# Output rows of a recurrent attention layer: three of four TensorE transposes given to a transposing DMA, with the output products of half 1 run block by block

## The chip, the cores and the metric

The kernel runs on one core of one Trainium2 chip. The metric is the device time of one execution in microseconds (us); lower is better. A comparison with the kernel before uses several executions of both on the same chip.

## The reference

Two layer pairs are applied to `x` (1 x 2048 x 448, bf16), one after the other with the same weights. The first of a pair is attention with a recurrent memory over segments of 32 tokens, the second a gated feed-forward layer; both add to their input, and both read it through a layer norm without weights.

```
for s in range(64):                       # 64 segments of 32 tokens
    h = concat([mem, x[32*s : 32*s+32]])  # 8 memory rows + 32 tokens = 40
    q, k, v = h @ Wq, h @ Wk, h @ Wv      # 16 heads of 256
    p = softmax(mask(q k^T / 16))         # memory columns open, tokens causal
    o = (p v) @ Wo                        # 40 x 448
    mem = o[:8]                           # into the next segment
    out[32*s : 32*s+32] = o[8:]
x = x + out
x = x + (relu(norm(x) @ W_gate) * (norm(x) @ W_up)) @ W_down
```

A segment needs the memory that the segment before left, so 64 segments of one layer follow each other.

## The kernel before

**Preparation.** Before the recurrence, `Wq Wk^T` of each head is made into `A_sb` and `Wv Wo` into `B_sb`, in 28 tiles for each half (8 heads) of the heads. Scores are then `(A_sb^T h)^T h`, and the output is `B_sb` times the weighted rows `Y`.

**Steps and chains.** The main loop (L1293) runs 68 steps. In step g chain 0 does segment g of the first attention layer and chain 1 segment g - 4 of the second (LAG = 4), so from g = 4 to 63 both chains are in each product's 80 columns. The feed-forward layer works on 128 rows, 64 of each chain (class `Feed`, L590), in the odd steps from 3 on. An odd step is long and an even one short. `early` (L1073) is an odd step with both chains.

**One step** (`step`, L902). `project` (L779) multiplies `hT` (the segment's rows turned, memory included) with `A_sb` of half 0 into five banks of PSUM in the order `BANKS` (L43); each bank is copied to `TQ` or `TZ` by DVE or ACT (L814). Then half 1 in the same way. `scores` (L931) makes memory scores (Sm) and token scores (Sx) of a half, `softmax` (L828) spreads their work over DVE and ACT as small closures (`[0]` first, `[1]` exp, `[2]` second, `[3]` lift, `[4]` peak, `[5]` rest), and writes the probabilities to `PJ`. They are turned either on TensorE (`flipped`, L873, tile pps) or by a DMA (`fetched`, L881, tile PT). `weigh_m` (L976) and `weigh_x` (L989) make `Y` of the memory rows and of the tokens, from the probabilities and `hk`, the segment's rows in their natural order. `hk` is itself a transposing DMA of `hT` (`turn_columns`, L893: two DMAs and a copy on POOL). `project_out` (L1023) multiplies `Y` with `B_sb` into `ox`, three blocks of 128 output columns, with the blocks inside the loop over the 28 tiles; `project_last` (L1031) makes the last 64 columns (o3). `finish` (L1056) copies the new memory from `ox` into `hT` of the next step and the token rows into `OT`. Behind it come the next step's early products (`project_early`, L764), which need only the last 64 columns, then `weigh_x` of half 0, then the first bank. `weigh_x` of half 1 runs inside the next step.

**Rows into the feed-forward layer.** `OT` holds the output with its columns on the partitions, in four blocks. In the odd step, behind the products of the first bank, `flip_rows` (L601) turns the four blocks on TensorE into the tile otp, `residual` (L606) adds them to `xa` on DVE and starts the row statistics, `norm` (L628) centres them into xn, `fetch` (L638) turns xn into `xT` by a DMA, and `squares` (L631) makes the row scale that `down_out` uses. `open_rows` (L647) is the first reader of `xT`.

**Order.** The wrappers at L85 and L100 keep each engine's instructions in the order in which the code emits them; only semaphores decide when. SP issues nearly all DMAs, in order. PSUM has eight banks; `bank` (L125) takes the one that a running estimate says has been free longest. In short steps with g % 4 = 2 (up to 54), `norm_rows` (L306) puts row statistics of later input rows on DVE between the copies of `project_last` and those of `finish`.

**The end.** After the loop the last 64 rows of the second layer are made in rows straight away (tile ot, L1309 to L1315), in two banks: even and odd tiles each fill one half of the array with 448 columns. `residual_of` (L610) copies one bank by ACT and adds it to the other by DVE.

Of the kernel before, what the change touches and what calls it, by code (L numbers as in the profile page):

```python
# [15 lines left out]
DM = 448  # L16
# [48 lines left out]
def build_kernel(ctx, tc, A_x, A_mem0, A_Wq, A_Wk, A_Wv, A_Wo, B_W_gate, B_W_up, B_W_down, out,  # L65
# [515 lines left out]
    nc.gpsimd.memset(OT[:], 0.0)  # L581
    xT = main.tile([P, 4, 128], BF, name="xT")
# [7 lines left out]
    class Feed:  # L590
# [188 lines left out]
    def project(hf, chains, hb, j, banks, pre={}, busy=False, first=None, inside=None, head=0, between=None):  # L779

        n = L * len(chains)
        for i0, k in banks:
# [110 lines left out]
    def turn_columns(g):  # L893

        if columns_by_dma(g):
            hk = HK[g % 2]
            src = hTb[g // BLK % 2][:, g % BLK, :]
            sp.dma_start_transpose(hk[:, 0:3, :], src[:, 0:3 * HI])
            sp.dma_start_transpose(hk[:, 3:4, 0:64], src[0:64, 3 * HI:HW])
            pool.tensor_copy(hk[:, 4, 64:128], hk[:, 3, 0:64])  # L900

    def step(g, ff, pre, late):  # L902
# [9 lines left out]
        end = g == nsteps - 1  # L912
        ox = None

        def ox_open():

            nonlocal ox
            ox = bank([P, 3, W], F32, "ox", 1400 if len(active(g + 1)) == len(chains) else 700, hold=True)
# [104 lines left out]
        def project_out(hf, t0, t1):  # L1023

            for t in range(t0, t1):
                for mc in range(3):
                    mm(ox[:, mc, lo:hi], B_sb[:, hf, t, mc * 128:(mc + 1) * 128],
                       YB[hf][:, t, lo:hi], start=(hf == 0 and t == 0 and mc == 0),
                       stop=(hf == 1 and t == NT - 1 and mc == 2), skip_group_check=True)

# [25 lines left out]
        def finish():  # L1056
            let_go(ox)
            if ms:
                src = ox[:, :, M0:M0 + 16].rearrange("p k (c m) -> p k c m", m=MEM)
                set_mem(g + 1, src[:, :, ms[0]:ms[-1] + 1, :], ms)  # L1060
            o = (g - 1) % BLK * SEG
            for c in xs:
                o2 = o + (TB if c == 0 else 0)
                dve.tensor_copy(OT[:, 0:3, o2:o2 + SEG], ox[:, :, XO[c]:XO[c] + SEG])

        def feed(*us):
            if ff is not None:
# [8 lines left out]
                between=(lambda: (ff.flip_rows(), ff.residual(), early and ff.norm())) if ff is not None else None)  # L1076
        project(0, chains, hb, j, BANKS[0][1:2], pre)
        hk = HK[g % 2] if columns_by_dma(g) else hk_make()
# [5 lines left out]
        if ff is not None:  # L1084
            if not two:
                ff.norm()
            ff.squares()
# [82 lines left out]
        if early:  # L1170
# [18 lines left out]
            px1 = fetched(PX[1], "x1")  # L1189
            ff.down()  # L1190
# [44 lines left out]
        else:  # L1235
# [7 lines left out]
            short = two and len(xs) == 1  # L1243
            if two:
                x1[3]()
            if not short:
                x0[0]()
                x0[1]()
            late_flip = NT if short else 23
            project_out(0, 0, late_flip)  # L1250
            pm = flipped(PM[1], 1, "m1") if ms else None
# [8 lines left out]
            straight = g <= LAG  # L1260
            if not straight:
                px0 = fetched(PX[0], "x0")
# [10 lines left out]
            flip = 25 if short else 10  # L1273
            project_out(1, 0, flip)
            if straight:
                px0 = flipped(PX[0], 2, "x0", act)
            project_out(1, flip, 25)
            next_piece()
            project_out(1, 25, NT)
# [29 lines left out]
    ot = [bank([P, 512], F32, "ot") for _ in range(2)]  # L1309
    mm(ot[0][0:TB, 0:DM], ident[:, 0:TB], ff.x[:], start=True, stop=False, tile_position=(0, 0), skip_group_check=True)  # L1310
# [78 lines left out]
```

## Time and profile before

| | us |
|---|---|
| median of 3 runs | 1521.43 |
| lowest, highest | 1520.22, 1522.34 |
| the profiled execution | 1520.04 |
| its span on the core | 1518.3 |

The profile is of one execution. PE is TensorE's matmuls, PEld its weight loads, DVE is VectorE, ACT ScalarE, POOL GpSimd, SP SyncE. A group's row reads: line, engine, operation, out<-in, shapes and count, then busy time in us, mean ns of one, idle time before it and what ended most of that idle time. A timeline row reads: start in us, length, engine, line, operation, count, and in brackets the idle time before it. Nearly all rows have line L107, L148 or L156, those of the wrappers, so tiles tell them apart. Matmuls overlap: a row's length runs to the end of its last one, and pace is read from one row's start to the next row's start. SPq rows are DMA issues; their length is the time that SP was held.

### The profile page before, as it was taken

To read this page: it belongs to the slowest core of one execution; us is meant where nothing else is said; L and a number is where in the kernel's file an instruction comes from. 1 tells how busy PE (TensorE), PEld (TensorE's weight loads), DVE (VectorE), ACT (ScalarE), POOL (GpSimd) and SP (SyncE) were. 2 spreads that over 40 slices of the span, in tenths; PEclk is the share of its full clock that TensorE was granted. 3 is DMA by queue.
4 is the path that set the end of the run, shared out by engine and by line. 5 is a ranking of instruction groups with operands and counts; after the bars stand their busy time and mean duration, and the time that the engine had idled before them with its cause. 6 is when DMAs were issued, how large, how long until landed. Compare 5 with 4: busy or idle time off the path is not lost.

```text
span 1518.3 us, 88540 instructions
## 1 busy us (share of the span) xinstructions
PE 1506.4 (99%) x40112; PEld 1396.0 (92%) x40112; DVE 1054.9 (69%) x3499; ACT 710.2 (47%) x1952; POOL 117.6 (8%) x234
## 2 busy tenths in 40 slices
PE   9999999999999999999999999999999999999998
PEld 6699999999999999999999999999999999999997
DVE  7766766777666677766677677666767776666664
ACT  6744444454444444544444445444444454444443
POOL 3301010101010010001001010100001000000000
PEclk9999999999999999999999999999999999999999
DMA  8721111111111111111111111111111111111100
GB/s 246 247 55 29 25 28 35 24 33 28 33 26 31 28 29 30 27 32 29 33 23 28 34 25 33 27 36 23 30 31 27 32 27 31 27 24 25 27 20 16
DMA packets 146250, 60.51 MB, mean 40 GB/s; under 512 B 119241, under 2 KB 144977, under 8 KB 145873
## 3 DMA queue, kind: packets, MB, share of 16 engines
q1 hardware_dynamic: 143744, 50.66, 14.6%
q8 instruction: 314, 5.14, 1.4%
q0 software_dynamic: 1088, 3.68, 0.7%
q14 instruction: 64, 0.52, 0.1%
q10 hardware_dynamic: 1040, 0.52, 0.1%
HBM read 23.18 MB, written 3.80 MB: 18 GB/s over the span
## 4 chain that ended last, share of the span: by engine, by line
PE 96%; DMA 3%; DVE 1%; issue 0%; ACT 0%; POOLq 0%; POOL 0%; SPq 0%; ACTq 0%
PE prj L148 32%; PE ox L148 25%; PE gps L148 6%; PE ups L148 6%; PE dps L148 6%; PE o L148 4%; PE y L148 4%; PE Sx L148 3%; DMA PT<-PJ 2%; PE Sm L148 1%; PE bps L148 1%; PE ya L148 1%; PE aps L148 1%; PE tpw L156 1%; PE yb L148 1%; PE otp L156 0%
## 5 line engine op out<-in xcount | busy, mean ns | idle before, releaser
L148 PE MATMUL prj<-hT,A_sb 128*128 128x80 bf16 (+3 forms) x15232 | 538.6, 199 | 0.4
L148 PEld LDWEIGHTS <-A_sb 128*128 128x128 bf16 (+1 forms) x15232 | 498.9, 99 | 20.8 <-issue 0.8
L148 PEld LDWEIGHTS <-B_sb 128*128 128x128 bf16 (+1 forms) x15008 | 472.5, 103 | 9.7 <-issue 2.1
L148 PE MATMUL ox<-Y,B_sb 128*128 128x80 bf16 (+2 forms) x11256 | 417.0, 200 | 1.5 <-issue 1.4
L107 ACT CAST Y<-y 128x128 bf16<-128x128 f32 (+2 forms) x452 | 150.3, 410 | 207.5 <-PE y L148 201.7
L107 ACT CAST TQ<-prj 128x480 bf16<-128x480 f32 (+1 forms) x380 | 184.5, 497 | 95.4 <-PE prj L148 83.8
L107 DVE CAST Y<-y 128x256 bf16<-128x256 f32 (+2 forms) x316 | 135.5, 479 | 42.5 <-PE y L148 42.0
L107 ACT ACTIVATE se<-se 128x160 f32<-128x160 f32 (+2 forms) x270 | 81.5, 302 | 166.4 <-DVE se L107 155.9
L148 PEld LDWEIGHTS <-Wg_sb 128*128 128x128 bf16 (+2 forms) x2128 | 124.5, 97 | 9.8 <-issue 2.7
L107 DVE CAST TQ<-prj 128x480 bf16<-128x480 f32 (+1 forms) x228 | 125.6, 572 | 8.0 <-PE prj L148 7.5
L148 PE MATMUL gps<-xT,Wg_sb 128*128 128x128 bf16 (+3 forms) x1904 | 128.7, 215 | 0.0
L148 PEld LDWEIGHTS <-hk 128*128 128x128 bf16 (+2 forms) x1950 | 101.0, 96 | 15.9 <-DMA PT<-PJ 2.8
L148 PE MATMUL ups<-xT,Wu_sb 128*128 128x128 bf16 (+3 forms) x1632 | 108.5, 215 | 0.4 <-DVE xT L107 0.4
L148 PEld LDWEIGHTS <-Wu_sb 128*128 128x128 bf16 (+1 forms) x1904 | 105.1, 97 | 1.7 <-issue 0.2
L107 ACT CAST TZ<-prj 64x320 bf16<-64x320 f32 (+2 forms) x264 | 96.5, 376 | 20.0 <-DVE TZ L107 16.0
L107 DVE TENSOR_REDUCE ssum<-se 128x4 f32<-128x160 f32 (+2 forms) x270 | 73.3, 271 | 42.1 <-ACT se L107 38.5
L107 DVE SCALAR_TENSOR_TENSOR hh<-gps,ut 128x512 bf16<-128x512 f32 (+2 forms) x136 | 80.4, 593 | 31.8 <-ACT ut L107 30.1
L148 PE MATMUL dps<-Wd_sb,hh 128*128 128x448 bf16 (+1 forms) x504 | 93.6, 342 | 0.8 <-DVE hh L107 0.7
L148 PEld LDWEIGHTS <-TQ 128*128 128x128 bf16 x1938 | 85.3, 96 | 4.6 <-ACT TQ L107 1.5
L148 PE MATMUL y<-PT,hk 40*128 40x256 bf16 (+3 forms) x1280 | 85.8, 248 | 1.7 <-DMA PT<-PJ 1.6
L107 DVE TENSOR_TENSOR PJ<-se,rs 128x160 bf16<-128x160 f32 (+2 forms) x270 | 76.1, 282 | 9.6 <-DVE rs L107 0.3
L107 ACT COPY os<-o 64x16 f32<-64x16 f32 (+3 forms) x134 | 25.7, 191 | 121.9 <-PE o L148 120.2
(142 smaller groups left out, 1612.5 us busy)
## 6 DMA issues: line engine op xcount, KB each, us to landing
wo<-in_A_Wo_dram POOLq DMA_DIRECT2D x8, 448.0 KB, 5.5
nat<-in_A_Wv_dram SPq DMA_DIRECT2D x8, 384.0 KB, 5.2
PT<-PJ SPq DMA_TRANSPOSE x160, 2.4
nat<-in_A_Wq_dram SPq DMA_DIRECT2D x6, 384.0 KB, 4.9
nat<-in_A_Wk_dram SPq DMA_DIRECT2D x6, 384.0 KB, 5.4
hk<-hT SPq DMA_TRANSPOSE x132, 3.1
dx<-ahead SPq DMA_DIRECT2D x15, 128.0 KB, 2.7
xp<-in_A_x_dram SPq DMA_DIRECT2D x16, 112.0 KB, 2.9
```

Of the source, the lines that this page charges most:

```text
L107: r = f(*a, **k)
L148: in_order(nc.tensor.matmul(out, lhsT, rhs, **k))
L156: in_order(nc.tensor.transpose(out, src, idn))
```

## The change

In the even steps from 4 to 62 (`turning`), half 1's output products run block by block: all 28 tiles of columns 128 to 255, then 256 to 383, then 0 to 127. The first two of these blocks have a PSUM tile of their own (ox2). When they are done, ACT copies their token rows to `OT`, one transposing DMA turns blocks 1 to 3 of `OT` (columns 128 to 447, with the 64 that project_last left) into the new tile `OR`, and DVE copies their memory rows to `hT`; then come the products of block 0. In the odd step behind it TensorE turns block 0 alone, and the residual is added in two parts, behind the copy of the first bank. The fetch of `xT` is issued ahead of the second bank and no longer behind the third, `squares` behind the softmax of half 1's tokens, and one TQ copy goes from DVE to ACT.

In short steps with both chains on both sides (`whole`) the exponential of x0 is emitted behind the turn of m1, x0's probabilities are written and fetched before x1's maximum, and ACT does the copies of m1's PT and of ya. The turn of m1 comes after 21 tiles of half 0 and no longer after 23. In steps 64 and 66 x0 is turned on TensorE and no longer by a DMA. POOL's copy for `hk` is emitted behind the second bank. At the end, each tile's product is split into two halves of 224 columns side by side in one bank, and ACT and DVE each copy one half to `xa`.

```diff
+        def flip_first(self):
+            self.rows = bank([P, 128], BF, "otp")
+            tr(self.rows[:], OT[:, 0, :], ident[:])
+
+        def residual_rows(self):
+            dve.tensor_tensor(self.x[:, 128:DM], OR[:].rearrange("p k d -> p (k d)")[:, 0:DM - 128], self.x[:, 128:DM],
+                              op=ALU.add)
+            dve.tensor_tensor(self.x[:, 0:128], self.rows[:], self.x[:, 0:128], op=ALU.add)
+            self.statistics(self.first)
...
         def residual_of(self, ot):
-            odd = main.tile([P, DM], F32, tag="odd", name="odd")
-            act.copy(odd[0:TB, :], ot[1][TB:P, 0:DM])
-            dve.tensor_tensor(self.x[0:TB, :], ot[0][0:TB, 0:DM], odd[0:TB, :], op=ALU.add)
+            for eng, r, cols in zip((dve, act), FR, HALF):
+                evac(eng, self.x[0:TB, cols], ot[r, 0:DM // 2])
...
-                copies(act if (i0 != 6 if busy and hf else i0 % 12) else dve, slice(0, P), T)
+                copies(act if (i0 != 6 if busy and hf else i0 if early else i0 % 12) else dve, slice(0, P), T)
...
+        turning = ff is None and g >= LAG and len(active(g + 1)) == 2
...
+            if turning:
+                a = bank([P, 1, W], F32, "ox", after, hold=True)
+                b = bank([P, 2, W], F32, "ox2", 700, hold=True)
+                ox = ((a, 0), (b, 0), (b, 1))
...
+        def project_out_rows(first):
+            o = (g - 1) % BLK * SEG
+            for mc in (1, 2, 0):
+                if mc == 0:
+                    src = ox[1][0]
+                    let_go(src)
+                    for c in xs:
+                        o2 = o + (TB if c == 0 else 0)
+                        act.copy(OT[:, 1:3, o2:o2 + SEG], src[:, :, XO[c]:XO[c] + SEG])
+                    sp.dma_start_transpose(OR[:], OT[:, 1:4, :].rearrange("p k t -> p (k t)"))
+                    put_mem(src, slice(1, 3))
+                    first()
+                for t in range(NT):
+                    mm(ox[mc][0][:, ox[mc][1], lo:hi], B_sb[:, 1, t, mc * 128:(mc + 1) * 128], YB[1][:, t, lo:hi],
+                       start=False, stop=(t == NT - 1), skip_group_check=True)
...
         project(0, chains, hb, j, BANKS[0][0:1], pre,
-                between=(lambda: (ff.flip_rows(), ff.residual(), early and ff.norm())) if ff is not None else None)
+                between=ff.flip_first if early else (lambda: (ff.flip_rows(), ff.residual())) if ff is not None else None)
+        if early:
+            ff.residual_rows()
+            ff.norm()
+            ff.fetch()
         project(0, chains, hb, j, BANKS[0][1:2], pre)
...
-        if early:
-            ff.fetch()
-        project(0, chains, hb, j, BANKS[0][3:5], pre, ff is not None)
+        project(0, chains, hb, j, BANKS[0][3:5], pre, ff is not None, early=early)
...
+            late_flip = NT if short else 21 if whole else 23
+            project_out(0, 0, late_flip)
+            pm = flipped(PM[1], 1, "m1", act if whole else dve) if ms else None
+            if whole:
+                x0[1]()
             if two:
                 x1[3]()
...
             project_out(0, late_flip, NT)
+            straight = not whole
+            if whole:
+                x0[2]()
+                px0 = fetched(PX[0], "x0")
             if two:
                 x1[4]()
-            weigh_m(1, hk, pm)
-            x0[2]()
+            weigh_m(1, hk, pm, act if whole else dve)
...
+            if turning:
+                next_piece()
+                project_out_rows(flip_x0)
...
         for t in range(NT):
-            r = slice(64 * (t % 2), 64 * (t % 2) + 64)
-            mm(ot[t % 2][r, 0:DM], YB[hf][:, t, XL:W], B_sb[:, hf, t, :], start=(hf == 0 and t == 1),
-               stop=(hf == 1 and t >= NT - 2), tile_position=(0, r.start), skip_group_check=True)
+            for r, cols in zip(FR, HALF):
+                mm(ot[r, 0:DM // 2], YB[hf][:, t, XL:W], B_sb[:, hf, t, cols], start=False,
+                   stop=(hf == 1 and t == NT - 1), tile_position=(0, r.start), skip_group_check=True)
```

More of the change, by code (lines that the diff above doesn't have):

```diff
@@ L581, in build_kernel @@
     nc.gpsimd.memset(OT[:], 0.0)
+    OR = main.tile([P, 3, 128], BF, name="OR")
     xT = main.tile([P, 4, 128], BF, name="xT")
@@ L777, in project_early, with project @@
         return pre
-    def project(hf, chains, hb, j, banks, pre={}, busy=False, first=None, inside=None, head=0, between=None):
+    def project(hf, chains, hb, j, banks, pre={}, busy=False, first=None, inside=None, head=0, between=None, early=False):
         n = L * len(chains)
@@ L912, in step @@
         end = g == nsteps - 1
+        px0 = None
+        turning = ff is None and g >= LAG and len(active(g + 1)) == 2
         ox = None
@@ L917, in ox_open @@
             nonlocal ox
-            ox = bank([P, 3, W], F32, "ox", 1400 if len(active(g + 1)) == len(chains) else 700, hold=True)
+            after = 1400 if len(active(g + 1)) == len(chains) else 700
+            if turning:
+                a = bank([P, 1, W], F32, "ox", after, hold=True)
+                b = bank([P, 2, W], F32, "ox2", 700, hold=True)
+                ox = ((a, 0), (b, 0), (b, 1))
+            else:
+                a = bank([P, 3, W], F32, "ox", after, hold=True)
+                ox = ((a, 0), (a, 1), (a, 2))
         def hk_make():
@@ L1026, in project_out, with put_mem @@
                 for mc in range(3):
-                    mm(ox[:, mc, lo:hi], B_sb[:, hf, t, mc * 128:(mc + 1) * 128],
-                       YB[hf][:, t, lo:hi], start=(hf == 0 and t == 0 and mc == 0),
+                    mm(ox[mc][0][:, ox[mc][1], lo:hi], B_sb[:, hf, t, mc * 128:(mc + 1) * 128],
+                       YB[hf][:, t, lo:hi], start=(hf == 0 and t == 0 and ox[mc][1] == 0),
                        stop=(hf == 1 and t == NT - 1 and mc == 2), skip_group_check=True)
+        def project_out_rows(first):
[13 more added lines that the diff above has]
+                       start=False, stop=(t == NT - 1), skip_group_check=True)
+        def put_mem(src, rows):
+            if ms:
+                src = src[:, :, M0:M0 + 16].rearrange("p k (c m) -> p k c m", m=MEM)
+                dve.tensor_copy(mem_of(g + 1, ms)[:, rows], src[:, :, ms[0]:ms[-1] + 1, :])
         def project_last():
@@ L1056, in finish @@
         def finish():
[L1057 to L1060, printed above, removed]
+            src = ox[0][0]
+            n = src.shape[1]
+            let_go(src)
+            put_mem(src, slice(0, n))
             o = (g - 1) % BLK * SEG
@@ L1189, in step @@
             px1 = fetched(PX[1], "x1")
+            ff.squares()
             ff.down()
@@ L1243, in step @@
             short = two and len(xs) == 1
+            whole = two and not short
+            if not short:
+                x0[0]()
+            if not two:
+                x0[1]()
[3 more added lines that the diff above has]
+            if whole:
+                x0[1]()
             if two:
                 x1[3]()
[L1246 to L1251, printed above, removed]
             if short:
@@ L1272, in step, with flip_x0 @@
             project_last()
[L1273 to L1279, printed above, removed]
+            def flip_x0():
+                nonlocal px0
+                if straight:
+                    px0 = flipped(PX[0], 2, "x0", act)
+            if turning:
+                next_piece()
+                project_out_rows(flip_x0)
+            else:
+                project_out(1, 0, 10)
+                flip_x0()
+                project_out(1, 10, 25)
+                next_piece()
+                project_out(1, 25, NT)
             if g % 4 == 2:
```

25 lines of the change are left out of this document (14 added, 11 removed).

## The prediction

> **What bounds the kernel now.** I read the page first: the busy line, the chain that ended last and the costliest groups.
>
> ```profile
> span 1518.3 us, 88540 instructions
> ...
> PE 1506.4 (99%) x40112; PEld 1396.0 (92%) x40112; DVE 1054.9 (69%) x3499; ACT 710.2 (47%) x1952; POOL 117.6 (8%) x234
> ...
> PE 96%; DMA 3%; DVE 1%; issue 0%; ACT 0%; POOLq 0%; POOL 0%; SPq 0%; ACTq 0%
> ...
> L148 PEld LDWEIGHTS <-hk 128*128 128x128 bf16 (+2 forms) x1950 | 101.0, 96 | 15.9 <-DMA PT<-PJ 2.8
> ```
>
> PE is busy 99% of the span and is 96% of the chain; the next engine, DVE, is at 69%. A busy PE may still be a PE with gaps between starts, so I then read PE's starts in the timeline over one seam, the end of a short step (g = 46) and the start of the long step behind it.
>
> ```profile
> 1058.69 3.18 PE L148 MATMUL ox<-Y,B_sb 128*128 128x80 bf16 x84
> 1061.81 0.60 PE L148 MATMUL prj<-hT,A_sb 64*128 64x80 bf16 x24
> 1062.25 0.65 PE L148 MATMUL y<-PT,hk 40*128 40x256 bf16 x10
> 1062.83 0.82 PE L148 MATMUL prj<-hT,A_sb 128*128 128x80 bf16 x18
> 1063.49 0.39 PE L156 MATMUL otp<-ident,OT 128*128 128x128 bf16 x4
> 1063.71 3.10 PE L148 MATMUL prj<-hT,A_sb 128*128 128x80 bf16 x85
> 1066.65 0.62 PE L148 MATMUL y<-PT,hk 40*128 40x256 bf16 x10
> 1067.09 0.31 PE L148 MATMUL prj<-hT,A_sb 64*128 64x80 bf16 x7
> ```
>
> The 84 ox products start over 3.12 us, 37 ns each, and nothing stands idle between the rows. I call 1061.81, the first early product of the long step, zero; below, +0.44 is the first weighing y (1062.25) and +4.84 the second (1066.65). The four transposes of the output rows hold PE from 1063.49 to 1063.71: 0.22 us, 0.055 each. So this kernel is bound by the number of instructions on PE; an edit is worth what it takes from PE's list, less any new wait at the head of PE's queue. Existing waits are few:
>
> ```profile
> PE y L148 <- DMA PT<-PJ: 1.6, 6, 0.4
> ```
>
> That is the first y of a long step waiting for the transposed probabilities of x0; on the weight loads the same wait is the 2.8 us of the page.
>
> **The change, part by part.** In the changed instruction order 30 short steps are affected (even g from 4 to 62, where both chains go on) and the 30 long steps behind them.
>
> *Transposes.* Each of the 30 long steps turns one block of the rows on PE and no longer four: 90 x 0.055 = 4.95 us less. Steps 64 and 66 now turn x0 on PE, two transposes each: 4 x 0.055 = 0.22 us more. The output products stay the same in number and shape; only their order changes, block by block. Products that follow each other into the same columns are not slower in this trace: prj does so four times in a row at (1066.65 - 1063.71) / 85 = 35 ns. I cost that edit at nothing; at 1 ns it would be 30 x 84 x 0.001 = 2.5 us.
>
> *x0's probabilities.*
>
> ```profile
> 1056.78 0.34 ACT L107 ACTIVATE se<-se 128x160 f32<-128x160 f32 x1 [1.80 <-DVE se L107]
> ...
> 1057.90 0.31 DVE L107 TENSOR_REDUCE ssum<-se 128x4 f32<-128x160 f32 x1
> ```
>
> The exponential ends at 1057.12, yet its sum starts at 1057.90, because DVE first copies m1's PT, takes x1's maximum and copies ya. In the changed order two of these go to ACT and one behind the sum. ACT has to copy the PT ahead of the exponential, about 0.2 us, so the sum and the DMA behind it come near 0.78 - 0.2 = 0.6 us sooner. That exceeds the longest wait of 0.4. I take 2.4 us of gain, most of the larger account, since the DMA that lands slowest could still be waited for a little; the bounds are 0 and 2.8.
>
> *DVE at the seam.*
>
> ```profile
> 1059.99 0.33 DVE L107 TENSOR_TENSOR PJ<-se,rs 128x160 bf16<-128x160 f32 x1
> 1060.23 0.37 DVE L107 TENSOR_TENSOR hT<-o,os 64x16 bf16<-64x16 f32 x2
> 1060.63 0.28 DVE L107 TENSOR_TENSOR OT<-o,os 64x32 bf16<-64x32 f32 x2
> 1060.84 0.61 DVE L107 BATCH_NORM_STATS2 stats<-xp 128x6 f32<-128x448 bf16 x1
> 1061.48 0.18 DVE L107 BATCH_NORM_AGGREGATE mv<-stats 128x2 f32<-128x6 f32 x1
> 1061.91 0.21 DVE L107 CAST hT<-ox 128x48 bf16<-128x48 f32 x1 [0.25 <-PE ox L148]
> 1062.04 0.41 DVE L107 CAST OT<-ox 128x96 bf16<-128x96 f32 x2
> 1062.70 0.69 DVE L107 CAST Y<-y 128x512 bf16<-128x512 f32 x1 [0.25 <-PE y L148]
> ...
> 1065.62 1.22 DVE L107 CAST TQ<-prj 128x480 bf16<-128x480 f32 x2
> ...
> 1067.10 1.22 DVE L107 CAST Y<-y 128x512 bf16<-128x512 f32 x3
> ```
>
> Now blocks 1 and 2 end 28 products, 1.04 us, before zero. ACT copies them into OT, and DVE's copy into hT stands behind ACT's. In the 13 short steps with g % 4 = 2 up to 54 the row statistics (0.61 + 0.18) queue behind that copy, where before they ran in DVE's idle time. With ACT's copies at -0.8 to -0.45, the hT copy to -0.27 and the statistics to +0.5, the last OT copy ends near +0.77 instead of +0.64 (1062.04 + 0.41). The y of chain 1 takes the bank of ox over, so it comes about 0.13 later: 13 x 0.13 = 1.7 us. In the 17 others the smaller last copies end earlier; I give back 0.04 each, 0.7. Together +1.0; bounds -0.7 and 13 x 0.3 = 3.9.
>
> *ACT takes a TQ copy from DVE.*
>
> ```profile
> 1062.72 1.48 ACT L107 CAST Y<-y 128x512 bf16<-128x512 f32 x5 [2.91 <-PE y L148]
> 1064.61 0.56 ACT L107 CAST TQ<-prj 128x480 bf16<-128x480 f32 x1 [0.41 <-PE prj L148]
> 1065.13 0.86 ACT L107 CAST TZ<-prj 64x320 bf16<-64x320 f32 x2
> 1066.47 0.56 ACT L107 CAST TQ<-prj 128x480 bf16<-128x480 f32 x1 [0.48 <-PE prj L148]
> ```
>
> ACT is free for 0.48 us between TZ (to 1065.99) and TQ; a copy of 0.56 goes there. TQ then ends up to 0.08 later than 1067.03, and PE's early products at 1067.09 take the bank of that copy. So 0 to 0.06 in 30 steps, 0 to 1.8 us; I take 0.5.
>
> *The transposing DMA and the residual.*
>
> ```profile
> 1058.81 3.06 SPq L107 DMA_TRANSPOSE PT<-PJ  x2
> 1062.15 3.11 SPq L107 DMA_TRANSPOSE hk<-hT  x2
> 1065.73 1.20 SPq L107 DMA_TRANSPOSE xT<-xn  x1
> ```
>
> ```profile
> PT<-PJ SPq DMA_TRANSPOSE x160, 2.4
> ...
> hk<-hT SPq DMA_TRANSPOSE x132, 3.1
> ```
>
> ```profile
> DMA to landing us min/median/max: 2.2/2.4/4.4
> ```
>
> The last line is of the tile PT. SP holds a transposing DMA for 1.2 us or more. The new one (OR) stands behind x1's PT, which now starts near -1.7, so OR issues between -0.45 and 0.5. In shape it is like the first of the two hk, and like them it has others close before and behind it: I take their median, 3.1, and land it near +2.7, between +1.8 and +4.9. The two hk move by about 1.2 us; their first readers come after the long step's memory softmax, far behind. xT is fetched later:
>
> ```profile
> 1063.91 0.39 DVE L107 TENSOR_TENSOR xa<-otp,xa 128x448 bf16<-128x448 bf16 x1 [0.52 <-PE otp L156]
> ...
> 1071.10 0.23 PE L148 MATMUL ups<-xT,Wu_sb 64*128 64x128 bf16 x1
> ```
>
> DVE now empties bank 0 first (half of the 1.22 row), to about +2.5, then adds the rows in two parts, takes statistics and centres. From the residual to xT's issue was 1.82 us; with a second add it is about 1.95. At the median landing OR ends hardly later than the bank copy: xn is ready near +4.6 (before +3.9), xT lands near +7.1, and PE reads it at +9.3 less 0.17. With OR at the maximum the chain ends at +6.8. Queued behind the residual on DVE is the second Y copy, for which PE is ready at +5.3 less 0.17, and PE takes its bank over about a microsecond later. That slack is gone when OR lands past about +3.5. I take one landing in four, by 0.27 us each: 30 / 4 x 0.27 = 2.0 us; bounds 0 and what the slower rival says.
>
> The Trainium skill, page VectorE: DVE Perf Modes, section The three transpose paths, lists 390 ns for a 128x128 bf16 transpose on TensorE and 1309 ns by the DMA crossbar, and its rules say to use TensorE where a PSUM destination will do. Taken at 390 each, 90 transposes would be 35 us by an estimate from that page; the trace shows 55 ns between starts, so the sum goes by 55. Read as advice it speaks against this change.
>
> *The end.*
>
> ```profile
> 1506.02 0.53 ACT L107 COPY odd<-ot 64x448 f32<-64x448 f32 x1 [2.87 <-PE ot L148]
> 1506.58 0.62 DVE L107 TENSOR_TENSOR xa<-ot,odd 64x448 bf16<-64x448 f32 x1 [4.62 <-ACT odd L107]
> ```
>
> 1.18 us in a row become two half copies side by side, some 0.4. The same columns go through PE. PE has other products under the first part of it; I take 0.3 of gain, bounds 0 and 0.8.
>
> **The sum.** The profiled execution took 1520.04 us (span 1518.3): -4.95 + 0.22 - 2.4 + 1.0 + 0.5 + 2.0 - 0.3 = -3.93, so 1516.1. The median of the three runs, 1521.43, lies 1.39 above the profiled run; put on the median the forecast is 1517.5.
>
> **Rivals.** *The gain comes back as waits.* The seam is packed: DVE's 0.13 at y and ACT's 0.06 at the early products together are as much as the 0.165 taken from a pair of steps. If both hit all 30 pairs at their upper bounds (3.9 + 1.8) and the x0 wait stays, the change is -4.95 + 0.22 + 5.7, about +1.0, and with half of those costs about -1.9: 1519.5 to 1522.5. Against it: the statistics run in 13 of 30 steps alone. *Slower: OR heads DVE's queue.* If OR regularly lands past +3.5, the residual holds everything behind it on DVE, and PE stands at the bank of the second Y copy, then at xT. At the maximum, +4.9, it is 1.4 us in each of 30 steps: 42 - 6 = 36 us more, 1557; at an average of 0.45 past the slack it is 13.5 - 5.9 = 7.6 more, 1529, which I give it. For it: SP's own issues sometimes take longer (3.06 for two), and OR queues behind one; hk's median is 0.7 above PT's. Against it: even 3.1 leaves 0.8 us. The Trainium skill's 1309 ns, in the section named above, would make three blocks in a row 3.9 us by an estimate; OR has as many blocks. The hk rows, two DMAs of which the first has three blocks, show a median of 3.1 for both kinds together, so blocks in a row are not excluded. *The turns were not on the path.* If PE's transposes sat in time that PE had to wait anyway, taking them away gives nothing: 1521. The starts in the seam, without an idle mark, speak against it.
>
> **How the numbers follow.** Forecast (1512 to 1518.4): 0.58. Gain eaten (0.18) or never there (0.07), 1518.4 to 1524.5: 0.25. Slower by OR: 0.17. The low end takes every gain and no cost: 1520.04 - 4.95 + 0.22 - 2.8 - 0.7 - 0.8 + 1.39 = 1512.4. The high end goes through the second case, to 1523.5, and leaves the slower rival out. 0.2% is 3.0 us, about what a measurement of this kernel can tell from no change; faster is the forecast's 0.58, same 0.25, slower 0.17.
>
> **What would show it.** Right: otp falls from 132 transposes to 42, no new row of PE waiting for DVE or ACT over 2 us in total, PE's y waiting for PT under 1 us, and the pair of steps shorter by about 0.17. Wrong: DVE's xa idle before OR's DMA for many microseconds together with PE waiting at y, prj or ups; hT<-ox landing late in the steps with statistics; TQ's end past PE's need. A wait of PE at prj right after zero, for DVE's hT, would break the forecast, since the recurrence passes there.

## The result, and the profile after

| | runs | median us | lowest, highest |
|---|---|---|---|
| before | 7 | 1522.34 | 1520.22, 1525.32 |
| after | 7 | 1516.65 | 1512.76, 1518.28 |

The ratio after to before is 0.9958, with a 95% interval of 0.9946 to 0.9971: about 0.42% less time, between 0.29% and 0.54%, which is 4.4 to 8.2 us. The forecast was 1517.5, a change of -3.93.

The profiled execution of after took 1517.59 us, 2.45 less than that of before. Its page, with the lines that answer those of before (a group's row has the busy time, the mean ns of one and the idle time before it):

```profile
span 1515.8 us, 88747 instructions
...
PE 1500.8 (99%) x40083; PEld 1392.6 (92%) x40083; DVE 1026.4 (68%) x3471; ACT 746.3 (49%) x2101; POOL 117.3 (8%) x234
...
PE 93%; DMA 4%; DVE 2%; issue 1%; ACT 0%; POOL 0%; SPq 0%; ACTq 0%; POOLq 0%
PE prj L148 31%; PE ox L148 25%; PE gps L148 6%; PE dps L148 6%; PE ups L148 6%; PE o L148 5%; PE y L148 4%; PE Sx L148 3%; DMA OR<-OT 2%; PE bps L148 1%; PE Sm L148 1%; PE ya L148 1%; PE yb L148 1%; PE tpw L156 1%; PE aps L148 1%; DMA nat<-in_A_Wk_dram 1%
...
L148 PEld LDWEIGHTS <-hk 128*128 128x128 bf16 (+2 forms) x1950 | 100.9, 96 | 13.2 <-issue 0.4
```

PE is still the bound, with 5.6 us less work, but its share of the chain of waits fell from 96% to 93%, and the new DMA, OR, stands in the chain with 2%. The weight loads of hk no longer name x0's transposing DMA as what they wait for. The waits (engine, line, what for: us in total, times, longest):

```profile
PE prj L148 <- DVE Y L107: 1.2, 4, 0.4
...
PE ups L148 <- DVE mx L107: 0.7, 1, 0.7
...
DVE hT L107 <- ACT OT L107: 19.5, 29, 0.7
...
DVE xa L107 <- DMA OR<-OT: 15.9, 20, 1.6
```

The row of PE's y waiting for PT is gone from this view. In its place PE's prj waits for DVE's copy of Y, and DVE waits 15.9 us for OR. The row of ups is in truth a wait for xT, as is shown at the end of this section. The same seam as was shown of before (the end of step 46), by the timeline (start, length, engine, operation, in brackets the idle time before it):

```profile
1060.03 0.33 ACT L107 CAST OT<-ox 128x64 bf16<-128x64 f32 x2 [1.41 <-PE ox L148]
1060.39 0.19 DVE L107 CAST hT<-ox 128x32 bf16<-128x32 f32 x1 [0.66 <-ACT OT L107]
1060.43 2.38 SPq L107 DMA_TRANSPOSE OR<-OT  x1
1060.50 0.62 DVE L107 BATCH_NORM_STATS2 stats<-xp 128x6 f32<-128x448 bf16 x1
1060.93 0.60 PE L148 MATMUL prj<-hT,A_sb 64*128 64x80 bf16 x24
...
1061.31 0.28 DVE L107 CAST OT<-ox 128x32 bf16<-128x32 f32 x2
1061.37 0.67 PE L148 MATMUL y<-PT,hk 40*128 40x256 bf16 x10
...
1061.97 0.82 PE L148 MATMUL prj<-hT,A_sb 128*128 128x80 bf16 x18
...
1062.62 0.22 PE L156 MATMUL otp<-ident,OT 128*128 128x128 bf16 x1
1062.68 3.10 PE L148 MATMUL prj<-hT,A_sb 128*128 128x80 bf16 x85
...
1063.97 0.33 DVE L107 TENSOR_TENSOR xa<-OR,xa 128x320 bf16<-128x320 bf16 x1 [0.49 <-DMA OR<-OT]
...
1065.61 0.55 PE L148 MATMUL y<-PT,hk 40*128 40x256 bf16 x8
...
1086.75 0.60 PE L148 MATMUL prj<-hT,A_sb 64*128 64x80 bf16 x24
```

Zero is 1060.93 here. The first y comes at +0.44, as before; the turn of one block takes 0.06 us where four took 0.22; the second y comes at +4.68 where it came at +4.84. The long step ends at 1086.75, so it is 25.82 us long. The same step of before ran from 1061.81 to 1087.79, 25.98 us. A step's length means this below: from one seam's early products to the next seam's.

By these seams the 2.45 us between the two profiles split as follows: the 30 long steps are 4.30 shorter, the first four steps 0.18 and the stretch after the last seam 1.10; the short steps are the same; the last three steps are 1.07 longer, and the preparation ahead of the first seam is 2.05 longer (84.65 before, 86.70 after). In the other kernels below, whose preparation has the same code, it ends between 84.38 and 85.43, so this profile caught a long one, and without it the profiles differ by 4.5 us.

The long steps fall into two kinds. Undisturbed they take 25.76 us behind a short step with g % 4 = 0 and 25.82 behind one with row statistics, against 25.98 of before. Some are longer. Step 30's seam shows why (zero is 713.79):

```profile
713.30 2.62 SPq L107 DMA_TRANSPOSE OR<-OT  x1
...
717.77 0.33 DVE L107 TENSOR_TENSOR xa<-OR,xa 128x320 bf16<-128x320 bf16 x1 [1.43 <-DMA OR<-OT]
...
719.55 1.22 DVE L107 CAST Y<-y 128x512 bf16<-128x512 f32 x3
...
720.29 2.67 PE L148 MATMUL prj<-hT,A_sb 128*128 128x80 bf16 x70 [0.20 <-DVE Y L107]
```

OR is issued at -0.49 but lands only at +3.96, 4.45 us later. DVE stands 1.43 us at the first add. Everything behind it on DVE is late, and PE stands at +6.50 for the bank that the Y copy frees. That step takes 26.18. What the tile OR shows in all 30 steps:

```profile
  DMA OR<-OT: 15.9, 20
...
DMA to landing us min/median/max: 2.3/3.2/4.4
```

Of the 15.9 us that DVE waits, PE pays only the end: 7 long steps show a pause of PE behind Sm, of 0.17 to 0.54 us, 2.5 in all. (The view of waits puts four of them down to the Y copy, with a part of each.)

The other new wait is at ups, the first reader of xT. In step 18 (zero is 453.54):

```profile
455.25 3.66 SPq L107 DMA_TRANSPOSE hk<-hT  x2
...
459.00 1.22 SPq L107 DMA_TRANSPOSE xT<-xn  x1
...
463.49 0.21 PE L148 MATMUL ups<-xT,Wu_sb 64*128 64x128 bf16 x1 [0.74 <-DVE mx L107]
```

xT is issued when SP is done with hk's two DMAs, lands at +9.81, and ups starts 0.14 later: PE waits for xT, though the view names DVE's mx. The step takes 26.64, 0.82 more than an undisturbed one. Before, xT was issued at +4.1 on average and landed at +9.0 at the latest; now it is issued at +5.0, and PE reads it at +9.07 or +9.13.

### The profile page after: what moved, and what is told of

It reads as the page before. It is cut to its first block, busy times and chain, and to the rows that moved or that the text cites. A ratio compares the mean times of both kernels' runs of the same rounds, so it can differ in the third digit from the quotient of the medians.

```text
span 1515.8 us, 88747 instructions
## 1 busy us (share of the span) xinstructions
PE 1500.8 (99%) x40083; PEld 1392.6 (92%) x40083; DVE 1026.4 (68%) x3471; ACT 746.3 (49%) x2101; POOL 117.3 (8%) x234
## 4 chain that ended last, share of the span: by engine, by line
PE 93%; DMA 4%; DVE 2%; issue 1%; ACT 0%; POOL 0%; SPq 0%; ACTq 0%; POOLq 0%
PE prj L148 31%; PE ox L148 25%; PE gps L148 6%; PE dps L148 6%; PE ups L148 6%; PE o L148 5%; PE y L148 4%; PE Sx L148 3%; DMA OR<-OT 2%; PE bps L148 1%; PE Sm L148 1%; PE ya L148 1%; PE yb L148 1%; PE tpw L156 1%; PE aps L148 1%; DMA nat<-in_A_Wk_dram 1%
## 5 line engine op out<-in xcount | busy, mean ns | idle before, releaser
L107 ACT CAST TQ<-prj 128x480 bf16<-128x480 f32 (+2 forms) x410 | 198.1, 501 | 74.8 <-PE prj L148 61.4
L107 DVE CAST TQ<-prj 128x480 bf16<-128x480 f32 (+1 forms) x198 | 108.9, 561 | 17.6 <-PE prj L148 17.1
```

The lines of the kernel that those rows point to most:

```text
L107: r = f(*a, **k)
```

## The experiments

**Theory.** The gain is 90 turns taken from PE, and x0's earlier fetch; what comes back of it is OR's landing, by the order of DVE's queue. **Rivals.** The turns were not on the path and the gain came from the new order; or the row statistics and ACT's copies at the seam cost as much as OR.

### Four turns again

```diff
-            self.rows = bank([P, 128], BF, "otp")
-            tr(self.rows[:], OT[:, 0, :], ident[:])
+            self.rows = bank([P, 4, 128], BF, "otp")
+            for kd in range(4):
+                tr(self.rows[:, kd, :], OT[:, kd, :], ident[:])
```

Blocks 1 to 3 are turned on TensorE again and not read; OR stays.

> The changed kernel, but TensorE again turns all four blocks of OT in the 30 long steps; three of the turned blocks are read by nobody, the residual still takes them from the transposing DMA. Theory (PE's list is the bound): 90 x 0.055 = 5.0 us come back, so about 0.3% more than the changed kernel, ratio to before near 0.999. Rival (the turns sat in time that PE had to wait anyway, and the gain came from the order around x0): nothing comes back, ratio 0.996.

Measured: 1520.22 us (11 runs), ratio to before 0.9986 (0.9977 to 0.9995), so 3.6 us above after by the medians, 4.3 by the two ratios, and the intervals do not meet. The seam of step 30 in its timeline:

```profile
715.87 0.60 PE L148 MATMUL prj<-hT,A_sb 64*128 64x80 bf16 x24
...
717.56 0.39 PE L156 MATMUL otp<-ident,OT 128*128 128x128 bf16 x4
717.79 3.10 PE L148 MATMUL prj<-hT,A_sb 128*128 128x80 bf16 x85
...
720.72 0.61 PE L148 MATMUL y<-PT,hk 40*128 40x256 bf16 x10
```

The four turns take 0.23 us and the second y comes at +4.85. The undisturbed long steps take 25.93 and 25.99, each 0.17 more than in after: 30 x 0.17 = 5.1 us. In sum the 30 steps of this profile are 4.7 us longer than after's, since the disturbed ones differ from execution to execution. The turns are on the path at their full price, and the rival that they were not falls.

### No wait for OR

```diff
+    OC = main.tile([P, 3, 128], BF, name="OC")
+    nc.gpsimd.memset(OC[:], 0.0)
...
-            dve.tensor_tensor(self.x[:, 128:DM], OR[:].rearrange("p k d -> p (k d)")[:, 0:DM - 128], self.x[:, 128:DM],
+            dve.tensor_tensor(self.x[:, 128:DM], OC[:].rearrange("p k d -> p (k d)")[:, 0:DM - 128], self.x[:, 128:DM],
```

The attention's output is left out of the residual in columns 128 to 447: zeros are added. OR's DMA still runs.

> The changed kernel, but the residual of the 30 long steps adds a tile of zeros in place of the rows that the DMA turns; the DMA is still issued. It leaves out 320 columns of the attention output. Theory (the DMA lands late in about 7 of 30 steps and holds DVE's queue): the waits of PE at the first products behind the memory scores go, 2.5 to 3.5 us less than the changed kernel, ratio near 0.994. Rival (those waits come from DVE's longer list itself): no difference, ratio 0.996, and the waits stay.

Measured: 1513.67 us, ratio 0.9945 (0.9931 to 0.9959). The interval overlaps that of after, so the times alone leave it open; the trace does not. Step 30's seam:

```profile
713.54 0.32 DVE L107 TENSOR_TENSOR xa<-OC,xa 128x320 bf16<-128x320 bf16 x1
...
716.21 1.22 DVE L107 CAST Y<-y 128x512 bf16<-128x512 f32 x3 [0.82 <-PE y L148]
...
717.20 2.67 PE L148 MATMUL prj<-hT,A_sb 128*128 128x80 bf16 x70
```

DVE now waits 0.82 us for PE at the Y copy, and PE's prj starts without a pause, 0.07 behind the last Sm at 717.13. No wait of prj for Y is left in this kernel's view of waits. Five long steps are still disturbed, by other DMAs (x0's PT in one, xT in two, and the layer's rows for hT in two). The long steps are 2.25 us shorter in sum than in after, with such other waits in both sums; the pauses behind Sm in after were 2.5, and all of them are gone here. So OR's lateness costs 2.3 to 2.5 us.

### OR one DMA later

```diff
+    OD = main.tile([P, 3, 128], BF, name="OD")
...
+                    sp.dma_start_transpose(OD[:], OT[:, 1:4, :].rearrange("p k t -> p (k t)"))
                     sp.dma_start_transpose(OR[:], OT[:, 1:4, :].rearrange("p k t -> p (k t)"))
```

A second transposing DMA of the same rows, which nobody reads, stands ahead of OR on SP.

> The changed kernel with one more transposing DMA of the same size on SP just ahead of the one that turns the rows, into a tile that nobody reads. The rows land about 1.2 us later, near +4.0 after the long step's first product on the average. Theory (slack ends at a landing of +3.5 after the first product): nearly every long step then waits, 0.5 to 0.9 us each, 15 to 25 us more than the changed kernel, ratio 1.006 to 1.013. Rival (there is more slack than that, the waits seen have another cause): under 3 us more, ratio 0.996 to 0.998.

Measured: 1552.54 us, ratio 1.0179 (1.0153 to 1.0205), 36 us more than after, above the 15 to 25 expected. Its waits:

```profile
PE y L148 <- DVE xa L107: 16.2, 18, 2.3
PE prj L148 <- DVE Y L107: 8.6, 25, 0.4
PE ups L148 <- DMA xT<-xn: 2.9, 5, 1.0
...
DVE xa L107 <- DMA OR<-OT: 66.1, 30, 4.1
```

The direction was right, the size too small. OR is issued 1.7 us later on average (-0.32 after zero in after, +1.36 here), because SP is held by the added DMA for 1.2 to 2.6 us, and it lands at +4.73 on average. All 30 long steps wait for it on DVE. The first row shows a wait that I had not named: the second y, due at +4.68, needs the bank in which otp stands, and that bank comes free only when the second add has read it, behind the wait for OR. So PE meets a late OR at two places, first at y and then, with what is left, behind Sm.

The two kernels together give a rule of this seam. Start of the first add after zero, and length of the long step, taken row by row from the two traces (steps without statistics):

| step | kernel | first add at | length us |
|---|---|---|---|
| 24 | after | +3.37 | 25.76 |
| 40 | after | +3.77 | 25.97 |
| 56 | after | +4.03 | 26.22 |
| 24 | OR later | +4.54 | 26.73 |
| 40 | OR later | +4.65 | 26.85 |

Up to about +3.56 an add costs nothing, and past it each microsecond costs one, wherever PE meets it (in steps with statistics from +3.62). With a mean start of the add at +4.75, that is 30 x 1.19 = 36 us. In seven steps a pause at ups comes on top, 3.8 us in all; the view puts two of them down to DVE's se, but in all seven ups starts 0.13 to 0.14 us behind xT's landing.

Steps 14 and 16 are 0.9 and 1.5 us longer than this gives, without a wait that accounts for it. There the granted clock was lower. The view of windows (start:end, length, then the busy time and instructions of PE, PEld, DVE, ACT and POOL, the granted clock, the DMA share and GB/s):

```profile
375.70:379.10 3.40, 1.11 (x37) 0.94 (x35) 1.05 (x3) 0.87 (x3) 0.00 (x0) 1.00 0.18 34
379.20:382.50 3.30, 3.30 (x57) 3.19 (x51) 2.73 (x12) 2.17 (x7) 0.24 (x1) 0.50 0.20 40
```

In step 14 PE pauses for 2.29 us up to 378.53; from 379.17 the granted clock is 0.50 for 3.41 us. The same stands behind the pauses of 1.75 in step 4 and of 1.70 in step 16, and behind none of the shorter ones, up to 1.47. So in these three steps the late row is paid twice. The runs differ with it: those with a mean clock of 0.996 to 0.998 took 1552.5 to 1554.5 us, those with 0.999 and 1.000 took 1546.4 and 1543.6. The profile is one of the former, and its long steps are 38.7 us longer in sum than after's.

### Row statistics ahead of the products

```diff
             if turning:
                 next_piece()
+                if g % 4 == 2:
+                    norm_rows((g + 6) // 4)
                 project_out_rows(flip_x0)
```

The call behind the products is left for the other steps.

> The changed kernel, but in the 13 short steps with row statistics these are emitted ahead of half 1's output products, so that on DVE they stand ahead of the copy of the new memory that waits for ACT. Theory: the long steps behind them lose 0.06 us each, 0.8 us in all, ratio about 0.0005 lower than the changed kernel's, at the edge of what can be told; in the trace the 25.82 us steps become 25.76. Rival (the 0.06 has another cause, such as POOL's work on those rows): the 25.82 stay.

Measured: 1516.20 us, ratio 0.9955 (0.9943 to 0.9968), not to be told from after. The seam of step 46, where DVE has done the statistics ahead of ACT's copy:

```profile
1057.85 0.61 DVE L107 BATCH_NORM_STATS2 stats<-xp 128x6 f32<-128x448 bf16 x1
1058.22 0.33 ACT L107 CAST OT<-ox 128x64 bf16<-128x64 f32 x2 [1.40 <-PE ox L148]
...
1059.56 0.61 PE L148 MATMUL y<-PT,hk 40*128 40x256 bf16 x10
...
1060.10 0.82 PE L148 MATMUL prj<-hT,A_sb 128*128 128x80 bf16 x18
```

From the first y to the products behind it PE takes 0.54 us here, as in after's steps without statistics, and 0.60 in after's step 46. All undisturbed long steps now take 25.76. The statistics cost after 13 x 0.06 = 0.8 us, which is real in the trace and too small for the times.

### Before with the new order of x0 alone

The short steps of before with x0's exponential, probabilities and fetch in the places that the changed kernel gives them, the turn of m1 after 21 tiles, and with ACT's copies of m1's PT and ya:

```diff
-            project_out(0, 0, late_flip)
-            pm = flipped(PM[1], 1, "m1") if ms else None
+            project_out(0, 0, late_flip)
+            pm = flipped(PM[1], 1, "m1", act if whole else dve) if ms else None
+            if whole:
+                x0[1]()
...
+            if whole:
+                x0[2]()
+                px0 = fetched(PX[0], "x0")
```

> The kernel before with one part of the change alone: in short steps the new order around x0 (its exponential behind the turn of m1, its probabilities fetched before x1's maximum, ACT copying m1's PT and ya). Theory: the waits of PE's first y for x0's probabilities go, 2 to 3 us less than before, ratio near 0.998; the turns are worth the rest. Rival (the order around x0 is where most of the 6 us come from): ratio near 0.996.

Measured: 1519.90 us, ratio 0.9987 (0.9976 to 0.9997): 2.0 us less than before. Of PE's y, this row of the waits is left:

```profile
PE y L148 <- DMA PT<-PJ: 0.7, 2, 0.4
```

The undisturbed long step stays at 25.98, and the 30 of them are 1.93 us shorter in sum. So this part does about what it was costed at, and nothing to the seam's other work. (The end of this profile, behind the last seam, is 3.0 us longer than in before: PE waits 2.20 us for xn there, and the granted clock is 0.50 for the 3.41 us that begin 1.3 us later. That is of one execution, and the 1.93 does not contain it.)

### The new end alone

Before with the output's last rows made in two halves of 224 columns in one bank, as in the diff of the change.

> The kernel before with the new end alone (each last product split into two halves in one bank, ACT and DVE each copying one half). Theory: 0.3 us less than before, up to 0.8: ratio 0.9995 to 1.0, not to be told from no change by time, but in the trace the stretch from the last early products to the end is 0.3 to 1.1 us shorter. Rival (224-column products cost more than 448-column ones): the stretch is longer.

Measured: 1522.38 us, ratio 1.0000 (0.9989 to 1.0011). The stretch after the last seam is 30.63 us, 0.24 less than in before and just under the 0.3 expected. From the last ot product to the end it is 12.44 where before has 12.65; in after it is 12.68, so there the new end gains nothing that the profile shows. The 1.10 us that after's stretch is shorter come ahead of it: before waits 0.33 us for x0's PT and 0.69 for xn in that stretch, and after for neither. After's own timeline shows that the two copies do not run side by side as I had it:

```profile
1503.43 0.38 DVE L107 CAST xa<-ot 64x224 bf16<-64x224 f32 x1 [4.04 <-PE ot L148]
...
1503.84 0.34 ACT L107 CAST xa<-ot 64x224 bf16<-64x224 f32 x1 [3.26 <-DVE xa L107]
```

ACT waits for DVE's copy, so they are some 0.8 in a row where before had 1.18. Whether it waits for the tile that both write or for the bank that both read was not tried.

### OR ahead of x1

In the steps in question x1's probabilities are fetched behind OR on SP and no longer ahead of it.

```diff
-            px1 = fetched(PX[1], "x1")
+            px1 = None if whole and turning else fetched(PX[1], "x1")
...
             def flip_x0():
-                nonlocal px0
+                nonlocal px0, px1
...
+                if whole and turning:
+                    px1 = fetched(PX[1], "x1")
```

> The changed kernel, but in short steps x1's probabilities are fetched behind the rows on SP's queue and no longer ahead of them. The rows then issue near -0.45 in every step, whatever x1's fetch takes. Theory: most of the 2.5 us of waits for the rows go, and x1's probabilities, needed at +4.7, land in time in nine of ten steps; 1 to 2 us less than the changed kernel, ratio near 0.995. Rival (landing times and not the place in the queue make the rows late): no difference, 0.996, or a loss of 1 us at the second y.

Measured: 1520.05 us, ratio 0.9981 (0.9970 to 0.9992), 3.4 us more than after; the intervals just touch, and the long steps of the profile are 3.2 longer in sum. Its waits:

```profile
PE ups L148 <- DMA xT<-xn: 2.2, 4, 1.3
PE ups L148 <- DVE se L107: 1.6, 2, 1.2
...
DVE xa L107 <- DMA OR<-OT: 10.5, 13, 2.2
```

OR comes sooner (DVE waits 10.5 us for it where it waited 15.9), but the gain does not reach PE: the second y now waits for x1's PT in three steps, and ups for xT in six, the longest pause 1.3 us. (The view puts two of the six down to DVE's se; ups starts 0.13 to 0.14 us behind xT's landing in all of them.) xT, further back on SP, is what loses: it is issued 0.94 us after xn is ready on average, where in after it was 0.11. The rival had seen the loss at y alone. **Both moves** together (statistics ahead of the products, and OR ahead of x1):

> The changed kernel with both: row statistics ahead of the products, and x1's probabilities fetched behind the rows. Theory: the two gains add, 2 to 3 us less than the changed kernel, ratio 0.994 to 0.995. Rival: no different from the changed kernel, 0.996.

Measured: 1521.92 us, ratio 0.9996 (0.9983 to 1.0009). The same waits, with 3.9 us of ups waiting for xT by the view alone. The longest, 2.31 us in step 12, is again followed by 3.41 us at a granted clock of 0.50, and that step takes 29.60. No better.

### hk's DMAs behind xT

The version with the statistics ahead, and in the long steps hk's two DMAs issued behind xT's:

```diff
-        turn_columns(g)
+        if not early:
+            turn_columns(g)
...
             ff.norm()
             ff.fetch()
+            turn_columns(g)
```

> The version with the row statistics ahead of the block-by-block products, and in the long steps the two hk DMAs issued behind xT's and no longer at the start of the step. SP then has nothing between OR and xT. Theory: only OR's own landing sets the second Y copy, and hk's DMAs matter to it merely as neighbours; the waits of PE at prj behind Sm stay as many (3 to 8 of 30) or become slightly fewer, hk is read past +13 and lands in time: 1514.5 to 1517 us, ratio 0.995 to 0.997. Rival: the hk DMAs beside OR are what makes it land at 3.5 to 4.4 us and no longer at 2.3; then the median landing falls from 3.2 towards 2.4, DVE's idle time before xa falls from 17 us to under 8, and 1 to 2 us more are gained. Against both: hk comes too late for the memory rows of half 0, and PE waits there.

Measured: 1521.74 us, ratio 0.9993 (0.9984 to 1.0002), 5.5 us more than the version that it starts from. OR's median landing stays at 3.3 us, so hk's DMAs are not what makes it late, and the rival falls. The loss comes mostly from elsewhere. Step 36 in its timeline:

```profile
848.79 1.19 SPq L107 DMA_TRANSPOSE xT<-xn  x1
...
850.03 3.96 SPq L107 DMA_TRANSPOSE hk<-hT  x2
...
854.08 4.60 SPq L107 DMA_TRANSPOSE PT<-PJ  x2
...
858.43 0.27 PE L148 MATMUL ya<-PT,hk 128*128 128x128 bf16 x2 [0.50 <-DMA PT<-PJ]
```

It was not hk that came too late, as I had put it, but what is queued behind hk on SP: the memory probabilities' PT starts at 854.08, 0.09 after hk's 3.96 us are over, and PE stands at ya. In eight long steps ya starts late like this, 3.7 us in all, where the long steps are 4.4 longer in sum than those of the version that it starts from. I had read SP's queue up to hk and not past it.

### Two blocks by the DMA

The same version with OR of two blocks (columns 256 to 447) and two turns on TensorE:

```diff
-            self.rows = bank([P, 128], BF, "otp")
-            tr(self.rows[:], OT[:, 0, :], ident[:])
+            self.rows = bank([P, 2, 128], BF, "otp")
+            for kd in range(2):
+                tr(self.rows[:, kd, :], OT[:, kd, :], ident[:])
...
-                    sp.dma_start_transpose(OR[:], OT[:, 1:4, :].rearrange("p k t -> p (k t)"))
+                    sp.dma_start_transpose(OR[:], OT[:, 2:4, :].rearrange("p k t -> p (k t)"))
```

> The version with the row statistics ahead of the block-by-block products, and only two blocks (columns 256 to 447) turned by the DMA, so two on TensorE. Theory: OR's landing does not grow with its blocks (xT with four blocks has a median of 2.5 us, OR with three 3.2), so it stays at a median of about 3.1 and the turns cost 30 x 0.055 = 1.65 us: about 1518, ratio 0.9965 to 0.998. Rival, blocks one after the other: the landing becomes a third shorter, near 2.2 in the median and under 3.5 at the most, the waits of PE at prj behind Sm go, and the 2 us that they cost pay for the turns: 1515.5 to 1516.5, ratio 0.995 to 0.996.

Measured: 1515.74 us (5 runs, 1514.67 to 1516.69), ratio 0.9955 (0.9942 to 0.9967). What the tile OR shows:

```profile
  DMA OR<-OT: 19.4, 20
...
DMA to landing us min/median/max: 2.3/3.2/4.4
```

The three landing figures are those of three blocks. So the rival, blocks one after the other, falls. The undisturbed long step takes 25.81 or 25.82, one turn (0.055) more than 25.76, which is the 1.65 us expected in 30 steps. The total time does not show it: this kernel, the one with the statistics ahead (1516.20) and after (1516.65) can't be told apart by their times. None of the versions tried is shown to beat after.

## Why the prediction was right, point by point

The forecast's own sum was -3.93 us, and the medians differ by 5.7, between 4.4 and 8.2. So the gain was put too small; that 1517.5 still lies within 0.9 of the measured 1516.65 owes something to luck, since the median of before rose from 1521.43 in three runs to 1522.34 in seven. The high end of 1523.5 has no working: the second case as added up there ends at 1522.5. The main mechanisms named are those that the traces show; the sizes:

| term | predicted | measured | by |
|---|---|---|---|
| turns off PE | -4.95 | -5.1 | e1: 0.17 in each long step |
| x0's probabilities | -2.4 | -1.9, -2.0 | e5, trace and medians |
| DVE and ACT at the seam | +1.5 | about -0.8 | undisturbed lengths |
| OR late | +2.0 | +2.3 | e2, long steps in sum |
| x0 turned in steps 64 and 66 | +0.22 | +0.11 in step 64 | seams |
| the end | -0.3 | -0.24, none in after | e7, after |
| xT late at ups | none | +0.8 | after, step 18 |

The first six add up to about -5.7, which is the difference of the medians, but that is no proof of them: they come from different kernels, and the two profiles, without the preparation, differ by 4.5. What the profile has besides is mainly the wait at ups and smaller waits of long steps for x0's PT and the layer's rows, 1.4 us in all. (e1, e2, e5 and e7 are the runs with four turns, without the wait for OR, with x0's order alone and with the end alone.)

*Transposes.* Right: the 55 ns between starts was the price. The Trainium skill's 390 ns, page VectorE: DVE Perf Modes, section The three transpose paths, does not appear as a cost on PE: here the row of one turn is 0.22 us long, but the next product starts 0.06 behind it. The rule of that page for TensorE (section Rules for kernel authors), weighed in the prediction as a case against the change, did not decide it. As for the 1309 ns listed there for the DMA, taken block by block they would make a landing of three blocks longer than one of two; the medians are 3.2 and 3.2.

*x0.* Right, and a little less than the 2.4. One such wait is left in after, at step 34, of some 0.3 us on PE's y.

*The seam.* The step of the prediction that failed, in size and sign: "Together +1.0", and ACT's 0.5. Steps without statistics are 25.98 - 25.76 = 0.22 shorter, 0.055 more than the three turns; steps with them 0.16, about the turns alone: together 17 x -0.055 + 13 x 0.005, about -0.9 by these lengths and -0.7 by those of the run with four turns. The 0.04 that I gave back for smaller last copies is there (y to prj takes 0.54 where it took 0.58), but statistics cost 0.02 against before and not 0.13, because ACT's two copies end at -0.57 and DVE's hT copy at -0.35, sooner than I placed them, and the last OT copy ends at +0.66, not at +0.77. ACT's extra TQ copy shows no pause of PE at the early products.

*OR.* Right in place, in kind and nearly in size: the slack ends near +3.56 (I had +3.5), and "one landing in four, by 0.27" became 7 of 30 clearly past it, by about 0.36 each. The median landing, read from hk's rows as 3.1, is 3.2. What I had named as a sign of being wrong, DVE's xa idle before OR for many microseconds with PE waiting at prj or ups, did appear, at a price of 2.5 and 0.8 us.

*xT.* Put at nothing outside the slower rival, with a landing near +7.1. In 29 of the 30 steps it cost nothing; in step 18 its own landing took 4.35 us and PE waited. It is the weak place of the new order: in the versions that made it later, the pauses at ups were 3.8 us (OR later), 3.7 (OR ahead of x1) and 7.0 (both moves).

*The slower rival.* Its mechanism is real, and the run with OR later shows it at full size: 30 steps at a mean of 1.19 us past the slack. Its price held too, a microsecond for a microsecond, with xT's pauses and three stretches of half the clock on top. What kept it away is where OR stands on SP: 1.7 us later it would have been true. It named the banks of the Y copy and xT; otp's own bank, where PE meets a late OR first, was missing, at no difference to the price.

*What the terms do not hold.* In the profile, step 66 is 0.92 us longer than in before, most of it two pauses of PE for which the trace names no wait, 0.7 and 0.4 us; other runs of the same loop show between 0.2 and 0.97 there. Their cause is open. What is lost there comes back behind the last seam in about the same size (1.10), where PE no longer waits for x0's PT and for xn.

## What to carry to other kernels

Where PE is full, a transpose is worth the gap that it makes between two starts of PE, not its own length; moved to a DMA, it gives back what the DMA's slow landings, not its median, take past the moment at which the instructions queued behind its reader are needed, here 2.5 of 5.1 us. On the issuing engine every DMA behind the moved one has to be read, not only the moved one: the two moves tried here lost more at DMAs further back on SP (xT in one, the memory probabilities' PT in the other) than they gained. A wait that the view of waits puts down to an engine is worth a look at the landings: the waits of ups for xT stood under DVE's name in fourteen steps of seven kernels.

## What the runs showed of the hardware

A transposing DMA of the same shape from the same place lands after 2.3 us in some steps and after 4.4 in others, and neither two blocks in place of three nor hk's DMAs out of its way changed that (medians 3.2, 3.2 and 3.3). The queue that issues it was held from 1.2 to 2.6 us for one. What sets a single landing stays open.

In these profiles the granted clock of TensorE fell to 0.50 for 3.41 us five times in the main loop and behind it (three in OR later, one in both moves, one at the end of x0's order alone). Each time PE had paused just before, for 1.70 to 2.31 us, and the fall began 0.1 to 1.8 us after the pause. Behind the other pauses, of up to 1.67 us, it stayed at 1.00. That the length of the pause decides was not tried on its own.

Matmuls into the same columns of a bank, 28 in a row, are not slower than matmuls that change the columns each time: the short steps, in which the output products changed from the one to the other, sum to the same length within 0.01 us.
